# A new order for the opening of an attention and gated-unit kernel, with buffers named in the plan

## The chip, the cores and the metric

The kernel runs on one core of a Trainium2 chip. A core has five engines that run their own instruction queues side by side: TensorE (PE, matrix products, written to PSUM), VectorE (DVE), ScalarE (ACT), GpSimd (POOL) and SyncE (SP, which here only issues DMA transfers). PEld in a profile is TensorE's loading of weights. The metric is the device time of one execution in microseconds (us). Before the change, the median of 3 runs is 304.27 us (304.13 to 304.36).

## What is computed

Eight batches of attention without softmax, normalised per head, feed a causal gated unit:

```python
kv = np.einsum('bhsd,bhse->bhde', k, v)          # 8 batches, 8 heads, 576 tokens, 64 wide
out = np.einsum('bhsd,bhde->bhse', q, kv)
rms = np.sqrt(np.mean(out * out, axis=-1, keepdims=True) + 1e-06)
x = out / rms * g_norm                            # then (b, s, h*d): 576 tokens x 512
for k in range(5):
    gate_pre += conv_w[k] * xp[:, k:k + S, :]     # causal convolution, xp is x padded in front
gate = 1 / (1 + np.exp(-gate_pre))
return (gate * (x @ w_val)) @ w_out
```

q, k, v and g_norm are 32-bit floats as they arrive; w_val, conv_w and w_out arrive as 64-bit words, which the kernel stages as pairs of 32-bit words and narrows itself.

## The kernel before, in words

The program is a list of about 1,240 small steps, the string `PLAN`. The last loop of the kernel walks through it and calls one function per step; each function issues a few instructions to one engine, or DMAs to one queue. There is no scheduler behind it: each engine executes its instructions in the order in which the plan has them, and waits only for data it reads and for buffers that others still use. So the place of a step in the plan sets what it is queued behind on its own engine, and nothing else does.

The tokens of a batch are split into chunks 0 to 3 of 128 tokens and chunk 4 of 64. The steps that matter for the opening, with their lines in the kernel before:

- `load_q_rows`, `load_half`, `stage_weight` issue loads: q by rows (L331; qs), halves of k and v (L312), weights as they arrive (L346). Batch 0's v and half of its q go through ACT's queue, the convolution weights (`cw`) through POOL's, all else through SP's.
- `start_warm n 256` issues n products of the identity with itself (L433), which nothing reads.
- `turn_q_rows b j` transposes chunk j of q on PE (L485 for batch 0, L491 for batch 1); `sort_q b j` copies it from PSUM into `qT`: four copies for batch 0 (L504, on DVE for chunks 1 and 2, on ACT for the others), one ACT copy for batch 1 (L500).
- `kv_product b i` forms half i of k^T v on PE (L445); for batch 0 `kv_half` copies it with four ACT copies into the block-diagonal `kv_bd` (L455), for batch 1 `kv_copy` copies it whole (L459).
- `narrow_weight w j n` is part n of narrowing weight tile j. Parts 0 (L365), 5 (L382) and 6 (L387) run on DVE and need only the staged words; parts 1, 2, 3 (L370, L372, L374) are an ACT chain behind part 0; parts 4 (L377) and 7 (L391) run on DVE. Part 7 of `wval` multiplies by the column `gcol`.
- `turn_cw` transposes the narrowed convolution weights together with g_norm on PE (L416) and `keep_cw` takes `cwT` (the taps) and `gcol` out of that PSUM bank with three DVE instructions (L420 to L422).
- `raw_half 0 c i` multiplies chunk c of q by half i of `kv_bd` (L533). A chunk's raw product is whole when both halves are in its bank. `square` (ACT, L552), `sums` (DVE, L565), `powers` (POOL, L573) and `normalise` (DVE for batch 0, L582) make x; `turn_x` (PE, L604) and `keep_x` (ACT, L611) put it into `xT` with tokens along the row. Batch 1 and later use `raw_pair` and `raw_tail` (L521), squares of L556 and ACT's normalise (L592).
- `halo` (POOL, L632) copies the ends of the blocks of `xT` that the convolution needs; `gate_start` (ACT, L636), `gate_tap` (DVE, L642) and `gate_end` (ACT, L649) make the gate; `val_product` and `keep_val` (PE L654, ACT L663) the value product of batches 0 and 1, `gated` (DVE, L667) their product. From batch 2 on, `val_fast` and `val_keep` (L703 to L724) and `fast_product` and `fast_keep` (L795, L805 to L818) form products from seven block products each in place of eight.

The order around the change is this part of the plan before; a number after a name is a batch, a chunk, a half or a part:

```python
turn_q_rows 0 3; turn_q_rows 0 2; turn_q_rows 0 0; turn_q_rows 0 1; turn_q_rows 0 4; sort_q 0 3; ...
narrow_weight cw 0 2; narrow_weight cw 0 3; start_warm 3 256; kv_product 0 0; sort_q 0 1; kv_half 0 0;
sort_q 0 4; narrow_weight cw 0 4; narrow_weight cw 0 7; start_warm 1 256; raw_half 0 3 0; raw_half 0 2 0;
raw_half 0 0 0; kv_product 0 1; turn_cw; keep_cw; kv_half 0 1; raw_half 0 1 0; raw_half 0 4 0;
```

Buffers that are used again come from pools: `psum.tile(..., tag="bank", bufs=8)` hands out the eight PSUM banks in turn, and other tags do the same in SBUF (`ot` 3 buffers, `gate` 3, `x` 2, `wexp` 2, `w64` 3). A step that takes a buffer waits until the last reader of what was in it is done.

Of the kernel before, what the change touches and what calls it, by code (L numbers as in the profile page):

```python
# [15 lines left out]
P = 128  # L16
# [3 lines left out]
load_q_rows 0 1; stage_weight cw 0; load_q_rows 0 0; load_half v 0 0; load_half k 0 0; load_half v 0 1;  # L20
load_half k 0 1; warm_up; stage_weight wval 1; stage_weight wval 0; start_warm 5 256; turn_q_rows 0 3;
turn_q_rows 0 2; turn_q_rows 0 0; turn_q_rows 0 1; turn_q_rows 0 4; sort_q 0 3; sort_q 0 2;
narrow_weight cw 0 5; narrow_weight cw 0 6; narrow_weight cw 0 0; sort_q 0 0; narrow_weight cw 0 1;
narrow_weight cw 0 2; narrow_weight cw 0 3; start_warm 3 256; kv_product 0 0; sort_q 0 1; kv_half 0 0;
sort_q 0 4; narrow_weight cw 0 4; narrow_weight cw 0 7; start_warm 1 256; raw_half 0 3 0; raw_half 0 2 0;
raw_half 0 0 0; kv_product 0 1; turn_cw; keep_cw; kv_half 0 1; raw_half 0 1 0; raw_half 0 4 0;
narrow_weight wval 1 5; narrow_weight wval 1 0; raw_half 0 3 1;
load_q_rows 1 1; narrow_weight wval 1 1; narrow_weight wval 1 6; narrow_weight wval 1 2; raw_half 0 4 1;
raw_half 0 2 1; load_q_rows 1 0; narrow_weight wval 0 0; narrow_weight wval 0 5; square 0 3; stage_weight wval 3;
narrow_weight wval 0 6; narrow_weight wval 1 3; sums 0 3; load_half k 1 0; square 0 2; square 0 4;  # L30
narrow_weight wval 0 1; narrow_weight wval 1 4; sums 0 2; narrow_weight wval 0 2; raw_half 0 0 1; raw_half 0 1 1;
powers 0 3; sums 0 4; narrow_weight wval 1 7; normalise 0 3; square 0 1; square 0 0; sums 0 1; sums 0 0;
turn_q_rows 1 2; turn_q_rows 1 0; turn_q_rows 1 3; narrow_weight wval 0 3; sort_q 1 0; turn_x 0 3;
turn_q_rows 1 4; sort_q 1 2; turn_q_rows 1 1; keep_x 0 3; narrow_weight wval 3 0; load_half v 1 0;
stage_weight wval 2; load_half k 1 1; load_half v 1 1; powers 0 2; sort_q 1 3; normalise 0 2;
narrow_weight wval 3 1; narrow_weight wval 0 4; normalise 0 4; narrow_weight wval 0 7; narrow_weight wval 3 5;
stage_weight wout 1; load_q 2 0; stage_weight wout 0; powers 0 1; turn_x 0 4; narrow_weight wval 3 2;
turn_x 0 2; load_half k 2 0; kv_product 1 0; load_q 2 2; stage_weight wout 2; normalise 0 0; normalise 0 1;
narrow_weight wval 3 3; keep_x 0 2; keep_x 0 4; narrow_weight wval 3 4; narrow_weight wval 2 0; turn_x 0 0;
narrow_weight wval 3 6; turn_x 0 1; val_product 0 1 1; keep_x 0 0; kv_product 1 1; keep_x 0 1;  # L40
narrow_weight wval 3 7; narrow_weight wval 2 5; gate_start 0 0; val_product 0 3 1; gate_start 0 3;
narrow_weight wval 2 1; halo 0; sort_q 1 4; kv_copy 1 1; sort_q 1 1; kv_copy 1 0; gate_start 0 1;
narrow_weight wval 2 2; raw_pair 1 3; gate_tap 0 0 3; gate_tap 0 0 2; gate_tap 0 3 3; narrow_weight wval 2 3;
gate_tap 0 3 2; gate_tap 0 0 1; narrow_weight wout 1 0; narrow_weight wout 1 5; narrow_weight wval 2 6;
narrow_weight wval 2 4; load_half v 2 0; load_half k 2 1; load_q 2 1; square 1 3; narrow_weight wout 1 1;
narrow_weight wout 1 2; raw_tail 1; load_half v 2 1; keep_val 0 1 1; val_product 0 0 0; square 1 2;
narrow_weight wval 2 7; keep_val 0 3 1; gate_tap 0 3 1; sums 1 3; gate_tap 0 0 0; narrow_weight wout 0 0;
gate_tap 0 1 3; sums 1 2; turn_q 2 0; powers 1 3; keep_val 0 0 0; gate_end 0 0; val_product 0 2 1;
val_product 0 0 1; powers 1 2; load_q 2 3; narrow_weight wout 1 3; square 1 4; normalise 1 3; sums 1 4;
narrow_weight wout 1 6; narrow_weight wout 1 4; gate_tap 0 1 2; keep_val 0 0 1; val_product 0 1 0; raw_pair 1 1;  # L50
normalise 1 2; powers 1 4; turn_x 1 3; square 1 0; val_product 0 2 0; narrow_weight wout 1 7; gated 0 0;
gate_tap 0 1 1; keep_val 0 1 0; normalise 1 4; narrow_weight wout 0 1; sums 1 0; gate_start 0 2; turn_x 1 4;
turn_x 1 2; val_product 0 3 0; square 1 1; keep_x 1 4; keep_x 1 3; keep_x 1 2; narrow_weight wout 0 5;
gate_tap 0 3 0; val_sums 0; narrow_weight wout 2 5; narrow_weight wout 2 0; powers 1 0; gate_tap 0 2 3;
gate_tap 0 2 2; narrow_weight wout 0 2; gate_tap 0 2 1; sums 1 1; narrow_weight wout 0 3; keep_val 0 2 0;
keep_val 0 3 0; keep_val 0 2 1; stage_weight wout 3; narrow_weight wout 0 4; narrow_weight wout 0 6;
gate_tap 0 1 0; narrow_weight wout 2 6; gate_end 0 3; kv_product 2 0; normalise 1 0; powers 1 1;
val_product 1 0 1; halo 1; val_product 1 1 1; kv_product 2 1; turn_x 1 0; normalise 1 1; keep_val 1 0 1;
turn_q 2 2; narrow_weight wout 0 7; gate_tap 0 2 0; gate_end 0 1; gate_end 0 2; val_sums 1; turn_q 2 1;
gated 0 3; gated 0 2; turn_x 1 1; val_product 1 3 1; load_q 3 0; keep_x 1 0; turn_q 2 3; load_q 3 1;  # L60
load_half v 3 0; load_half v 3 1; narrow_weight wout 2 1; kv_copy 2 1; keep_x 1 1; weight_sums 0; val_sums 2;
gate_start 1 1; val_product 1 1 0; kv_copy 2 0; keep_val 1 1 1; narrow_weight wout 2 2; gate_tap 1 1 3;
keep_val 1 3 1; narrow_weight wout 2 3; narrow_weight wout 3 0; raw_pair 2 3; narrow_weight wout 3 5;
gate_tap 1 1 2; gated 0 1; square 2 2; square 2 3; keep_val 1 1 0; gate_start 1 0; narrow_weight wout 3 1;
raw_pair 2 1; val_product 1 0 0; narrow_weight wout 3 2; val_product 1 3 0; narrow_weight wout 3 3;
narrow_weight wout 3 6; token_sums 0 0 0; sums 2 3; val_product 1 2 1; val_product 1 2 0; powers 2 3; sums 2 2;
turn_q 3 0; token_sums 0 0 1; narrow_weight wout 3 4; square 2 1; keep_val 1 0 0; keep_val 1 3 0; load_q 3 3;
narrow_weight wout 3 7; narrow_weight wout 2 4; narrow_weight wout 2 7; load_half k 3 0; load_q 3 2;
load_half k 3 1; powers 2 2; fast_product 0 0 0; sums 2 1; normalise 2 3; token_sums 0 0 2; turn_blocks 2 3;
normalise 2 2; square 2 0; turn_q 3 1; powers 2 1; gate_start 1 3; fast_product 0 1 0; fast_product 0 0 1;  # L70
fast_keep 0 0 0; keep_val 1 2 0; normalise 2 1; weight_sums 1; raw_tail 2; sums 2 0; gate_tap 1 0 3;
fast_keep 0 0 1; fast_product 0 0 2; fast_keep 0 0 2; powers 2 0; square 2 4; keep_val 1 2 1; fast_keep 0 1 0;
weight_sums 2; token_sums 0 0 3; fast_product 0 0 3; fast_product 0 0 5; turn_blocks 2 2; turn_blocks 2 1;
sums 2 4; fast_keep 0 0 5; gate_tap 1 0 2; normalise 2 0; fast_product 0 0 4; fast_product 0 1 2; powers 2 4;
fast_keep 0 1 2; store 0 0; normalise 2 4; turn_blocks 2 0; move_blocks 2 0; move_blocks 2 2; move_blocks 2 1;
kv_product 3 0; fast_keep 0 0 4; turn_q 3 2; gate_tap 1 0 1; gate_tap 1 0 0; weight_sums 3; turn_q 3 3;
fast_product 0 1 4; turn_x 2 4; fast_product 0 1 1; kv_product 3 1; keep_x 2 4; kv_copy 3 0; kv_copy 3 1;
fast_product 0 0 6; move_blocks 2 3; raw_pair 3 3; raw_pair 3 1; gate_tap 1 3 3; load_half v 4 0; load_q 4 0;
gate_end 1 0; fast_keep 0 1 1; square 3 3; fast_keep 0 0 6; square 3 1; fast_product 0 1 3; fast_product 0 1 5;
gate_tap 1 3 2; gated 1 0; fast_keep 0 1 4; gate_tap 1 1 1; val_fast 2 0 0; sums 3 3; sums 3 1; gate_tap 1 1 0;  # L80
fast_keep 0 1 5; square 3 0; fast_product 0 1 6; square 3 2; sums 3 2; x_sums 2 0; gate_end 1 1; val_fast 2 1 0;
powers 3 3; x_sums 2 1; x_sums 2 3; gate_tap 1 3 1; gate_tap 1 3 0; val_fast 2 0 1; val_keep 2 0 0;
val_fast 2 0 2; x_sums 2 2; val_sums 3; sums 3 0; gated 1 1; fast_keep 0 1 6; val_keep 2 1 0; normalise 3 3;
val_keep 2 0 2; powers 3 2; powers 3 1; gate_end 1 3; val_fast 2 1 2; val_fast 2 1 1; load_half k 4 0;
val_keep 2 1 2; gate_start 1 2; val_keep 2 0 1; val_fast 2 0 4; gate_tap 1 2 3; val_keep 2 1 1; gate_tap 1 2 2;
val_fast 2 1 4; val_fast 2 0 5; val_fast 2 1 5; load_half v 4 1; normalise 3 2; load_half k 4 1; val_keep 2 0 4;
# [783 lines left out]
```

## Time and profile before

| what | value |
|---|---|
| median of 3 runs | 304.27 us |
| the profiled execution's own time | 305.54 us |
| its span, first to last instruction | 303.8 us |
| granted TensorE clock, mean | 0.995 |
| PE busy | 293.9 us (97% of the span) |
| DVE busy | 273.0 us (90%) |
| ACT busy | 194.4 us (64%) |
| POOL busy | 114.5 us (38%) |
| DMA | 55.51 MB, mean 183 GB/s |

The span is 1.7 us shorter than the profiled execution's own time; what lies around it is start and end of the program. The busy times are unions of instructions, so two that overlap count once. PE's busy time includes the products of `start_warm`, and a matmul that waits for its weights in mid-stream still counts as busy. In a timeline line stand the start, the time covered, the engine, the source line, the operation, what it writes and reads, and how many instructions are merged; a bracket gives the idle time before it and what ended that.

### The profile page before, as it was taken

What the parts mean: (1) busy time and instruction counts of PE and PEld (TensorE: products, weight loads), DVE (VectorE), ACT (ScalarE), POOL (GpSimd) and SP (SyncE); (2) the same over time, 40 slices, a digit from 0 to 9 for tenths busy, and PEclk for the clock granted to TensorE, in tenths of its full rate; (3) what the DMA queues carried; (4) which work ended last, traced back from release to release, by engine and by line L of the source; (5) the groups of instructions that cost most, each with busy time, mean ns of one, the idle gap of its engine ahead of it and who ended that gap; (6) DMA issues with size and microseconds to landing.
All of it is one profiled execution on the core that took longest, in us unless ns stands there. A gap on an engine that the chain in (4) does not pass through costs nothing.

```text
span 303.8 us, 8778 instructions
## 1 busy us (share of the span) xinstructions
PE 293.9 (97%) x3333; PEld 226.6 (75%) x3333; DVE 273.0 (90%) x482; ACT 194.4 (64%) x606; POOL 114.5 (38%) x127
## 2 busy tenths in 40 slices
PE   7998999999999999999999999999999999999993
PEld 4787777777887885777778757787877578888582
DVE  1699999999999999999999999999999999999612
ACT  2799989989568654983586537682888354534220
POOL 3047074326549036265328452245535613000000
PEclk9999999999999999999999999999999999999997
DMA  7999995277559776988589477937411621112423
GB/s 269 397 398 340 271 296 144 58 242 223 165 134 332 212 187 147 286 233 247 153 249 299 125 175 214 311 101 222 108 38 37 175 68 36 35 46 61 104 69 104
DMA packets 32073, 55.51 MB, mean 183 GB/s; under 512 B 6166, under 2 KB 14358, under 8 KB 32032
## 3 DMA queue, kind: packets, MB, share of 16 engines
q1 hardware_dynamic: 29520, 49.76, 56.6%
q0 software_dynamic: 1632, 3.17, 4.0%
q10 hardware_dynamic: 880, 2.03, 1.8%
q8 instruction: 26, 0.43, 0.6%
q14 instruction: 15, 0.12, 0.1%
HBM read 39.21 MB, written 9.44 MB: 160 GB/s over the span
## 4 chain that ended last, share of the span: by engine, by line
PE 76%; DMA 8%; SPq 5%; ACT 4%; DVE 3%; issue 2%; DVEq 0%
PE a L795 15%; PE va L703 13%; PE cb L795 12%; PE val L654 11%; PE vc L703 6%; PE kvps L445 4%; PE raw L521 4%; DMA out_dram<-ot 4%; PE out L741 4%; PE vb L703 3%; DMA qs<-in_q_dram 3%; SPq L625 2%; PE xTps L604 2%; DMA v<-in_v_dram 2%; SPq L322 1%
## 5 line engine op out<-in xcount | busy, mean ns | idle before, releaser
L573 POOL TENSOR_TENSOR rt<-ss,mhalf 128x8 f32<-128x8 f32 (+3 forms) x38 | 68.5, 1810 | 101.0 <-DVE ss L565 100.8
L642 DVE SCALAR_TENSOR_TENSOR gate<-xT,cwT,gate 128x576 f32<-128x576 f32 x128 | 101.8, 809 | 1.0
L592 ACT ACTIVATE x<-raw,rt 128x64 f32<-128x64 f32 x252 | 55.9, 353 | 6.9 <-POOL rt L573 4.1
L625 POOL DMA_DIRECT2D xT<-y x48 | 26.4, 557 | 25.9 <-DVE ot L805 14.4
L654 PE MATMUL val<-xT,wval 128*128 128x288 f32 x128 | 33.4, 412 | 0.0
L795 PE MATMUL a<-wsum,sums 128*128 128x256 f32 x128 | 32.5, 383 | 0.0
L649 ACT ACTIVATE gate<-gate 128x576 f32<-128x576 f32 x32 | 22.0, 692 | 12.1 <-DVE gate L642 11.9
L654 PEld LDWEIGHTS val<-xT,wval 128*128 128x128 f32 x128 | 23.5, 190 | 6.9 <-DVE wval L391 0.5
L795 PEld LDWEIGHTS a<-wsum,sums 128*128 128x128 f32 x128 | 23.9, 190 | 4.4 <-issue 0.6
L556 ACT ACTIVATE sq<-raw 128x256 f32<-128x256 f32 (+1 forms) x70 | 22.1, 402 | 7.8 <-PE raw L521 7.5
L703 PE MATMUL va<-xs,vsum 128*128 128x288 f32 x96 | 26.6, 409 | 0.0
L636 ACT ACTIVATE gate<-xT,cwT 128x576 f32<-128x576 f32 x32 | 25.2, 810 | 1.4 <-DVE gv L667 1.3
L565 DVE TENSOR_REDUCE ss<-sq 128x8 f32<-128x520 f32 (+1 forms) x40 | 24.7, 627 | 0.8 <-ACT sq L556 0.7
L667 DVE TENSOR_TENSOR gv<-gv,gate 128x576 f32<-128x576 f32 x32 | 23.6, 750 | 0.9 <-ACT gate L649 0.8
L703 PEld LDWEIGHTS va<-xs,vsum 128*128 128x128 f32 x96 | 18.0, 190 | 5.2 <-ACT x L592 0.4
L632 POOL COPY xT<-xT 128x124 f32<-128x124 f32 x32 | 17.5, 585 | 10.9 <-ACT xT L611 10.9
L521 PEld LDWEIGHTS raw<-kv,qT 64*64 64x64 f32 x1008 | 16.7, 134 | 6.4 <-issue 3.5
L521 PE MATMUL raw<-kv,qT 64*64 64x64 f32 x1008 | 19.0, 221 | 0.9 <-DVE gv L710 0.6
L445 PEld LDWEIGHTS kvps<-v,k 64*64 64x64 f32 x1008 | 15.8, 135 | 4.1 <-issue 2.9
L445 PE MATMUL kvps<-v,k 64*64 64x64 f32 x1008 | 17.4, 220 | 0.0
L470 DVE STREAM_TRANSPOSE qT<-qs 128x512 f32<-128x512 f32 x24 | 16.6, 693 | 0.5 <-DMA qs<-in_q_dram 0.5
L805 DVE TENSOR_TENSOR ot<-cb,ot 128x512 f32<-128x512 f32 x16 | 10.9, 681 | 6.8 <-DMA out_dram<-ot 4.1
(114 smaller groups left out, 545.5 us busy)
## 6 DMA issues: line engine op xcount, KB each, us to landing
qs<-in_q_dram SPq DMA_DIRECT2D x96, 140.0 KB, 4.6
out_dram<-ot SPq DMA_DIRECT2D x140, 64.0 KB, 1.7
k<-in_k_dram SPq DMA_DIRECT2D x14, 576.0 KB, 6.7
v<-in_v_dram SPq DMA_DIRECT2D x12, 576.0 KB, 7.0
xT<-y SPq DMA_DIRECT2D x48, 64.0 KB, 2.7
xT<-y POOLq DMA_DIRECT2D x48, 64.0 KB, 3.1
y<-in_moe_w_val_dram SPq DMA_DIRECT2D x4, 512.0 KB, 11.4
w_wout<-in_moe_w_out_dram SPq DMA_DIRECT2D x4, 512.0 KB, 7.1
```

Source lines behind the costliest of these rows:

```text
L445: nc.tensor.matmul(st["kvps", b][s][r * D:(r + 1) * D, i], st["k", b, i][rows, r, cols], st["v", b, i][rows, r, cols], start=(j == 0), sto ...
L521: nc.tensor.matmul(st["raw", b, c][r][cols, to * D:(to + 1) * D], st["qT", b][rows, hp, first:first + D], kvs[b % 2][rows, hp, :], start=T ...
L565: nc.vector.reduce_sum(out=st["ss", b][:, FIRST[c]:FIRST[c] + n], in_=st["sq", b, c][:, 0:n], axis=AX.X)
L573: nc.gpsimd.tensor_tensor(out=st["rt", b][:, which], in0=st["ss", b][:, which], in1=mhalf[:, which], op=ALU.pow)
L592: nc.scalar.activation(out=x[:, to * D:(to + 1) * D], in_=raw[:, h * D:(h + 1) * D], func=AF.Copy, scale=root[:, to:to + 1])
L625: (nc.sync if i % 2 else nc.gpsimd).dma_start(out=xTs[b % 2][i * TB:(i + 1) * TB, :, first:first + P], in_=y[a * TB:(a + 1) * TB, i])
L636: nc.scalar.activation(out=gate[:], in_=xTs[b % 2][:, jt, HALO:SX], func=AF.Copy, scale=cwT[:, K - 1, jt:jt + 1])
L642: nc.vector.scalar_tensor_tensor(out=gate[:], in0=xTs[b % 2][:, jt, tap * TB:tap * TB + S], scalar=cwT[:, tap, jt:jt + 1], in1=gate[:], op ...
L654: nc.tensor.matmul(val[:], wval[:, kc, jt * P:(jt + 1) * P], xTs[b % 2][:, kc, HALO + n * SV:HALO + (n + 1) * SV], start=(kc == 0), stop=( ...
L667: nc.vector.tensor_tensor(out=both, in0=both, in1=st["gate", b, jt][:], op=ALU.mult)
L703: nc.tensor.matmul(st[bank, "val", b, mj][:], weights_[:, k], tokens()[:, k], start=(n in (0, 1, 3) and k == 0), stop=(k == NK // 2 - 1), ...
L795: nc.tensor.matmul(st[bank, i, p], tokens()[:, k], weights_[:, k], start=(n < 2 and k == 0), stop=(k == NK // 2 - 1), skip_group_check=True)
```

## The change

Two things change. First, the plan: it has the same steps, each as often as before, in another order. In the opening, chunk 1 of q is turned first and chunks 3 and 2 last; `turn_cw` stands ahead of `kv_product 0 1` in place of behind it, and `keep_cw` right behind that product; the sort of chunk 3 stands behind the first `kv_half`; all raw halves stand behind `kv_product 0 1`, the two halves of chunk 4, of chunk 0 and of chunk 1 next to each other; the loads of batch 1 and of the weights change places on SP's queue, and `halo 0` stands ahead of three of the `keep_x 0` steps. Later parts of the plan are re-ordered as well, nearly everywhere by a few places; the last stores keep their queues.

Second, the buffers: the pools are replaced by tiles that are made once, and a step that takes a buffer names which one behind an `@`. The number of buffers of each kind stays. The warming products take a bank of their own each time, where they shared one before.

```diff
-turn_q_rows 0 2; turn_q_rows 0 0; turn_q_rows 0 1; turn_q_rows 0 4; sort_q 0 3; sort_q 0 2;
-narrow_weight cw 0 5; narrow_weight cw 0 6; narrow_weight cw 0 0; sort_q 0 0; narrow_weight cw 0 1;
-narrow_weight cw 0 2; narrow_weight cw 0 3; start_warm 3 256; kv_product 0 0; sort_q 0 1; kv_half 0 0;
-sort_q 0 4; narrow_weight cw 0 4; narrow_weight cw 0 7; start_warm 1 256; raw_half 0 3 0; raw_half 0 2 0;
-raw_half 0 0 0; kv_product 0 1; turn_cw; keep_cw; kv_half 0 1; raw_half 0 1 0; raw_half 0 4 0;
...
+stage_weight cw 0 @ 0; turn_q_rows 0 1 @ 1; turn_q_rows 0 4 @ 0; sort_q 0 1 @ 0; turn_q_rows 0 0 @ 2;
+sort_q 0 4; turn_q_rows 0 3 @ 3; turn_q_rows 0 2 @ 4; sort_q 0 0; start_warm 3 256 @ 0; load_q_rows 1 1;
+load_q_rows 1 0; narrow_weight cw 0 0 @ 0; narrow_weight cw 0 5 @ 0; narrow_weight cw 0 1; sort_q 0 2;
+stage_weight wval 3; kv_product 0 0 @ 1 2; narrow_weight cw 0 2; load_half k 1 0; narrow_weight cw 0 3;
+load_half v 1 0; start_warm 1 256 @ 0; narrow_weight cw 0 6 @ 1; narrow_weight cw 0 4; kv_half 0 0;
+narrow_weight cw 0 7; sort_q 0 3; turn_cw @ 4; kv_product 0 1; keep_cw; load_half k 1 1; stage_weight wval 2;
+raw_half 0 3 0 @ 3; narrow_weight wval 1 5 @ 1; kv_half 0 1; load_half v 1 1; narrow_weight wval 1 0 @ 0;
+raw_half 0 2 0 @ 4; narrow_weight wval 1 6 @ 0; narrow_weight wval 1 1; raw_half 0 3 1;
+narrow_weight wval 0 5 @ 2; raw_half 0 2 1; stage_weight wout 1 @ 0; square 0 3 @ 0;
+narrow_weight wval 0 6 @ 1; raw_half 0 4 0 @ 1; narrow_weight wval 1 2; sums 0 3 @ 0 0; raw_half 0 4 1;
+square 0 2 @ 1; raw_half 0 0 0 @ 2; narrow_weight wval 0 0 @ 1; stage_weight wout 0 @ 1; powers 0 3;
+square 0 4 @ 0; raw_half 0 0 1; sums 0 2; narrow_weight wval 1 3; raw_half 0 1 0 @ 0; sums 0 4; square 0 0 @ 1;
+raw_half 0 1 1; narrow_weight wval 1 4; turn_q_rows 1 2 @ 5; load_q 2 2; square 0 1 @ 0; sums 0 0; powers 0 2;
...
-    loads = ctx.enter_context(tc.tile_pool(name="loads", bufs=2))
-    work = ctx.enter_context(tc.tile_pool(name="work", bufs=2))
+    ROOMS = {"w64": (3, 1024), "ot": (3, 512), "wexp": (2, 512), "gate": (3, 576), "xs": (4, 576), "x": (2,
+             512), "qT": (2, 2304), "k0": (1, 1152), "k1": (1, 1152), "v0": (1, 1152), "v1": (1, 1152), "ss": (2,
+             36), "rt": (2, 36), "sq": (2, 520)}
+    rooms = {tag: [const.tile([P, size], FP32, name=f"{tag}_{n}") for n in range(count)]
+             for tag, (count, size) in ROOMS.items()}
+    rooms["bank"] = [psum.tile([P, 512], FP32, name=f"bank{n}") for n in range(8)]
+    picked = []
+    def new(tag, shape, dtype, name):
+        room = rooms[tag][picked.pop(0)]
...
     def ps(shape, name):
-        return psum.tile(shape, FP32, tag="bank", bufs=8, name=name)
+        return new("bank", shape, FP32, name)
...
         for step in PLAN.split(";"):
+            step, _, places = step.partition("@")
             name, *args = step.split()
+            picked[:] = [int(n) for n in places.split()]
             steps[name](*[int(a) if a.isdigit() else a for a in args])
```

Two switches that the diff adds change nothing here: `ACT_SUMS` is empty, and `PAIRED_Q` holds batch 0 as `WHOLE` did.

## The prediction, as it was put on record

> **What bounds the kernel now.** I read the page first, then the windows, the waits, and the timelines of the opening. The page's chain of waits is TensorE (PE) work for three quarters; the busy row beside it says the same, with VectorE (DVE) close behind:
>
> ```profile
> PE 293.9 (97%) x3333; PEld 226.6 (75%) x3333; DVE 273.0 (90%) x482; ACT 194.4 (64%) x606; POOL 114.5 (38%) x127
> ...
> PE 76%; DMA 8%; SPq 5%; ACT 4%; DVE 3%; issue 2%; DVEq 0%
> ```
>
> An average hides the stages, so I cut the span into windows (columns: length, then busy time and count of PE, PEld, DVE, ACT, POOL; granted clock; DMA share; GB/s):
>
> ```profile
> 8.00:16.00 8.00, 7.92 (x178) 5.87 (x177) 4.95 (x17) 6.04 (x21) 0.00 (x0) 1.00 1.06 398
> 16.00:24.00 8.00, 7.08 (x84) 5.97 (x83) 7.72 (x16) 7.34 (x14) 4.51 (x3) 1.00 1.05 398
> ...
> 28.60:64.00 35.40, 35.02 (x603) 27.05 (x601) 35.19 (x62) 32.98 (x96) 12.42 (x12) 1.00 0.74 198
> 64.00:176.00 112.00, 111.31 (x1422) 86.21 (x1423) 110.15 (x190) 78.11 (x272) 56.34 (x63) 1.00 0.76 215
> 176.00:284.00 108.00, 107.50 (x866) 83.79 (x864) 103.92 (x169) 60.62 (x187) 35.39 (x40) 1.00 0.42 114
> 284.00:298.70 14.70, 14.65 (x68) 10.60 (x64) 5.11 (x10) 3.00 (x8) 0.00 (x0) 1.00 0.33 85
> ```
>
> From 28.6 to 298.7 us PE is idle for 0.38+0.69+0.50+0.05 = 1.6 us in all: there the kernel is bound by PE, whose instructions the change keeps in number and shape. DVE is nearly as full there (idle 0.2 of 35.4 us, then 1.9 of 112). After 298.7 come 5.1 us of last copy and stores, which keep their engines and order. What can be moved is when the full stretch begins. PE before it:
>
> ```profile
> 12.01 1.83 PE L533 MATMUL raw<-kvbd,qT 128*128 128x128 f32 x12
> 13.77 1.28 PE L445 MATMUL kvps<-v,k 64*64 64x64 f32 x72
> 14.98 0.23 PE L416 MATMUL cwps<-ident,cw 21*128 21x21 f32 x1
> 15.14 4.05 PE L533 MATMUL raw<-kvbd,qT 128*128 128x128 f32 x28
> 19.12 2.84 PE L491 MATMUL qTps<-ident,qs 128*64 128x128 f32 x48
> 22.42 0.63 PE L604 MATMUL xTps<-ident,x 128*128 128x128 f32 x4 [0.46 <-ACT sq L552]
> 23.51 1.58 PE L491 MATMUL qTps<-ident,qs 128*64 128x128 f32 x24 [0.47 <-ACT qT L500]
> 25.65 0.85 PE L604 MATMUL xTps<-ident,x 128*128 128x128 f32 x6 [0.56 <-ACT wexp_wval L370]
> 26.43 1.28 PE L445 MATMUL kvps<-gv 64*64 64x64 f32 x72
> 27.64 1.11 PE L604 MATMUL xTps<-ident,x 128*128 128x128 f32 x8
> 28.58 2.11 PE L654 MATMUL val<-xT,wval 128*128 128x288 f32 x8
> ```
>
> The first value product starts at 28.58; before it PE waits three times (0.46+0.47+0.56) for the normalisation chain. That chain is late because DVE stood still: the convolution weights were ready at 12.51, but their turning sat on PE behind three raw halves and the second k^T v:
>
> ```profile
> 12.23 0.28 DVE L391 SCALAR_TENSOR_TENSOR cw<-ot_cw,wexp_cw 20x128 f32<-20x128 f32 x1
> 15.25 0.16 DVE L420 TENSOR_SCALAR gcol<-cwps 128x1 f32<-128x1 f32 x1 [2.73 <-PE cwps L416]
> ...
> 15.78 0.42 DVE L382 TENSOR_SCALAR ot_wval<-y 128x512 uint32<-128x512 uint32 x1
> ```
>
> **The change part by part**, times from the span's start; instructions of a kind are equal in number, so I walk the new order with the durations of these rows.
>
> *First loads and turned q.* The first eleven loads keep their queues and order; q lands at 6.0 to 6.2 and PE starts at 6.05. Chunk 1 is turned first and sorted by DVE from 7.2 (4 x 0.43) to 8.95. ACT sorts the small chunk 4 (4 x 0.27) and chunk 0 (4 x 0.375) from 7.5 to 10.1. The weight loads are in by then (issued 2.68, 5.8 us to landing). ACT's three weight steps (0.43 apart) end at 11.4; DVE does its first two, chunk 2 (1.73), then its last three, and ends at 12.06 against 12.51.
>
> *Turning the weights ahead of the second k^T v.* PE waits for them to 12.1. Behind that wait stands the second k^T v, whose k half lands at 12.09 (issued 1.68, 10.4 us); v's landing isn't told, but its other half took 0.2 us longer than k's (8.1 against 7.9), so I take 12.3. Bounds: nothing, or, if v lands only at 13.77, where the row above used it, some 1.5 us on this product and, less ACT's cover below, about 1 us on the end. I take nothing. keep_cw (three short rows, 0.62 from 15.25 to 15.87) runs 12.35 to 12.97, and DVE's next work waits for the value weights, landing at 2.19+11.2 = 13.4 and 2.98+11.7 = 14.7: a new wait of 0.4, in place of 2.7. DVE starts on them 2.4 us earlier (13.4 against 15.78).
>
> *Chunk 3's sort behind kv_half.* On ACT: kv_half 0 to 12.35 (4 x 0.22), chunk 3's sort to 13.88, kv_half 1 (0.87) to 14.77, against 15.97. The first raw half therefore waits to 13.95, against 12.01. This is the change's cost: PE idles 0.45 and has done no raw half before the second k^T v.
>
> *Raw halves in a row.* Ten halves at 0.57 (28 records in 3.98) are 5.7 us: 13.95 to 19.65, against an end of 19.12. PE is 0.5 later, yet chunk 3 is whole at 15.7 instead of about 16.8, and its square comes at 15.8 instead of 18.07, the last square ends at 20.2 instead of 22.3. POOL's three powers (2.07, 2.32, 2.89) end near 24.4 instead of 26.65; DVE's last normalise near 26.4 instead of 27.97.
>
> *PE to the value product.* From 19.65: 72 records of turned q at 0.059 (4.26), 18 of turned x at 0.117 (2.1, from 8 in 0.94) and one k^T v (1.21) are 7.57: 27.2. ACT has, from 20.2, three steps for weight 0 (0.75+0.65+0.63), three sorts (0.47 each), three steps of weight 3 (0.65+0.6+0.65) and three copies of turned x (0.5+0.35+0.5): 6.7, to 26.9. So PE, ACT and DVE meet within half a microsecond, and the three PE waits vanish because the chain is now 1.5 to 2.3 us earlier. The value product starts at 27.2: 28.58-27.2 = **1.4 us won**. What is late next is PE's own work.
>
> *Loads moved on SP's queue.* k and v of batch 1 and two value weights change places, the first two output weights go ahead of q of batch 2. DMA share is over 1.0 up to 48 us, so no load comes sooner by itself. The tightest: v's second half landed at 17.06+10.7 = 27.8, wanted at 29.2; the first output weight at 18.37+12.0 = 30.4, wanted by DVE near 31.6. I cost this at nothing; a slip past these margins costs its excess.
>
> *Halo 0 on POOL* moves ahead of three copies of x, to about 25.8, beside DVE's weight 3. In before it ran at 27.87, and the DVE row beside it took 0.81 where it takes 0.68: 0.13 each, three or four rows, 0.5 us of DVE, which is 1.5 us ahead.
> The Trainium skill, SBUF — State Buffer, section "SBUF: two separate sides", speaks against this: DVE work with two SBUF inputs and GpSimd work that reads SBUF share a port pair, and the loser "fully blocks". By it the four halo copies (2.1 us) would hold DVE outright; the 0.81 us row and the powers, beside which rows kept their 0.68, say they do not.
>
> *Everything after, and the places.* Both the rest of the order and the buffers are new: PSUM banks were taken in turn by a pool, now each has a number written out. Reading the list, a dozen banks are rewritten after only 0.86 to 1.2 us of PE work. An ACT copy takes 0.37 and the idle before it up to 0.22, so each fits with 0.3 to spare. The trace doesn't show these picks: at best all 1.6 us of PE idle go; at worst a dozen waits of 0.2 to 0.6 (PE's longest such wait is 0.6, a raw product waiting for DVE) cost 2.4 to 7 (the far end only if ACT is behind at all of them). I take zero, the row nearest: PE was stalled 1.6 us in 270.
>
> **Sum.** The profiled execution took 305.54 with a span of 303.8; the median of the runs is 304.27. Span 303.8-1.4 = 302.4; on the median 304.27-1.4 = **302.9 us**.
>
> **Rivals.**
> - *Middle gains too* (302.9-1.6 = 301.3): DVE gains 2.4 us of start against PE's 1.4, so the PE waits on DVE could go. For: the 0.6 wait is on DVE. Against: most of the rest is handover.
> - *The gain is given back* (304.3): DVE and ACT are 99% and 93% full up to 64 us; if a tight step there comes late, PE catches up with them. The halo as a full block belongs here: 2.1 us off DVE's 1.5 us lead leaves 304.3 or so. By that skill page this would be the outcome; the 0.13 says otherwise, so it has little weight.
> - *Slower: a hand-picked bank is still being read* (304.3-1.4+2.4 = 305.3 for twelve waits of 0.2). It decides once ACT's backlog passes 0.3 us at these places. For: the picks are tight. Against: ACT is only 56 to 70% busy after 64 us.
> - *It does not do what it says* (304.3): the weights are turned early, but DVE finds no value weights; against it stands their landing at 13.4.
>
> **Chances.** Forecast 0.42 (302.3 to 303.6), middle gains 0.23, given back 0.13, does nothing 0.04, slower 0.18. A measurement of this kernel tells about 0.2% (0.6 us) from no change. Faster 0.65, within 0.17, slower 0.18. The range reaches from 301.2 (all PE waits gone) to 305.3 (twelve bank waits); beyond it lie about 2 in 10.
>
> **What would show it.** In the changed profile: the weights' matmul near 12.1 and before the second k^T v; DVE's first value-weight row at 13.4; the last raw half at 19.6; no PE idle of 0.4 or more between 19.6 and 27; the value product at 27.2; PE idle from there to its end still near 1.6. A value product after 28 breaks the walk; PE waits on ACT copies after 64 us would be the slower rival.

## The result, and the profile after

| kernel | median | runs | ratio to before, 95% interval |
|---|---|---|---|
| before | 304.33 us | 303.71 to 304.63 (8) | |
| after | 305.53 us | 304.57 to 306.31 (8) | 1.0041, 1.0024 to 1.0058 |

The change makes the kernel 0.4% slower: 1.2 us lost where 1.4 were forecast as won, and just above the range. Two executions among the runs below, one of plan_pools (499.36 us, granted clock 0.56, the profiled one) and one of before (339.08 us, 0.853), are left out of the comparisons. The profiled execution of after took 305.46 us, with a span of 303.6. Its busy row and its chain of waits, from the page:

```profile
PE 292.6 (96%) x3333; PEld 226.0 (74%) x3333; DVE 273.0 (90%) x482; ACT 194.5 (64%) x606; POOL 112.5 (37%) x127
...
PE 70%; DMA 12%; DVE 9%; SPq 4%; issue 2%; ACT 1%; DVEq 0%; ACTq 0%
```

The sums hardly differ from before's; what moved is the chain, where DVE and DMA have more and PE less. PE's timeline of the opening answers to the one shown in the prediction:

```profile
12.05 0.23 PE L451 MATMUL bank<-ident,cw 21*128 21x21 f32 x1
12.48 1.28 PE L476 MATMUL bank<-v,k 64*64 64x64 f32 x72 [0.20 <-DMA v<-in_v_dram]
13.89 4.63 PE L563 MATMUL bank<-kvbd,qT 128*128 128x128 f32 x40
19.46 2.84 PE L521 MATMUL bank<-ident,qs 128*64 128x128 f32 x48 [0.94 <-DMA qs<-in_q_dram]
...
27.22 2.11 PE L698 MATMUL bank<-xT,wval 128*128 128x288 f32 x8
```

The weights are turned at 12.05 (forecast 12.1), the raw halves start at 13.89 (13.95), the value product at 27.22 (27.2). So at these three places the opening did what was forecast, and the loss is behind it. The windows, columns as in the prediction:

```profile
28.60:64.00 35.40, 34.84 (x604) 27.40 (x604) 35.33 (x62) 32.78 (x96) 11.12 (x10) 1.00 0.77 220
64.00:176.00 112.00, 110.25 (x1414) 85.00 (x1415) 108.56 (x186) 76.89 (x270) 56.52 (x64) 1.00 0.74 211
176.00:284.00 108.00, 107.41 (x866) 83.69 (x864) 103.70 (x169) 60.79 (x186) 34.54 (x39) 1.00 0.42 113
```

From 64 to 176 us PE idles 1.75 us (0.69 before) and DVE 3.4 (1.9 before); the later stretches hardly differ. From 28.6 to 298.7 us PE idles about 3 us in all; the prediction's last sign was that it would stay near 1.6. PE's own list of waits (us in all, times, longest) names, after 64 us, two of 0.6 that before did not have, both on an ACT copy:

```profile
PE bank L747 <- ACT gv L758: 0.6, 1, 0.6
PE bank L838 <- ACT ot L850: 0.6, 1, 0.6
```

They look like the slower rival, a PSUM bank that ACT has not yet emptied. The first of them, on the timeline of after (L711 is `gated`, L680 `gate_start`, L758 the copy that empties a bank of the value product, L747 `val_fast`):

```profile
94.75 0.74 DVE L711 TENSOR_TENSOR gv<-gv,gate 128x576 f32<-128x576 f32 x1
...
95.53 0.77 ACT L680 ACTIVATE gate<-xT,cwT 128x576 f32<-128x576 f32 x1 [1.78 <-DVE gv L711]
96.21 0.68 ACT L758 COPY gv<-bank 128x288 f32<-128x288 f32 x2
96.34 1.67 DVE L686 SCALAR_TENSOR_TENSOR gate<-xT,cwT,gate 128x576 f32<-128x576 f32 x2 [0.84 <-ACT gate L680]
96.64 0.54 PEld L747 LDWEIGHTS bank<-xT,vsum 128*128 128x128 f32 x3 [1.10 <-ACT gv L758]
96.64 0.75 PE L747 MATMUL bank<-xT,vsum 128*128 128x288 f32 x2 [0.65 <-ACT gv L758]
```

Read upwards: PE waits for ACT's copy, which is late only because it stands behind a `gate_start` that waited 1.78 us for DVE to finish `gated`. That is an SBUF tile: gate (1, 2) (batch, column tile) is written into the tile of gate (1, 1), and `gated 1 1` is the last to read it. The bank is where the wait is seen, not where it comes from.

### The profile page after: what moved, and what is told of

It reads as the page before. It is cut to its first block, busy times and chain, and to the rows that moved or that the text cites. A ratio compares the mean times of both kernels' runs of the same rounds, so it can differ in the third digit from the quotient of the medians.

```text
span 303.6 us, 8765 instructions
## 1 busy us (share of the span) xinstructions
PE 292.6 (96%) x3333; PEld 226.0 (74%) x3333; DVE 273.0 (90%) x482; ACT 194.5 (64%) x606; POOL 112.5 (37%) x127
## 4 chain that ended last, share of the span: by engine, by line
PE 70%; DMA 12%; DVE 9%; SPq 4%; issue 2%; ACT 1%; DVEq 0%; ACTq 0%
PE bank L838 29%; PE bank L747 23%; DMA qs<-in_q_dram 9%; PE bank L785 5%; PE bank L698 4%; PE bank L551 4%; DVE gate L686 3%; PE bank L476 3%; DMA k<-in_k_dram 2%; SPq L669 2%; DMA out_dram<-ot 2%; PE bank L648 1%; SPq L358 1%; PE bank L521 1%; PE bank L515 1%
## 5 line engine op out<-in xcount | busy, mean ns | idle before, releaser
L617 POOL TENSOR_TENSOR rt<-ss,mhalf 128x8 f32<-128x8 f32 (+3 forms) x38 | 68.0, 1794 | 100.3 <-DVE ss L607 100.3
L636 ACT ACTIVATE x<-bank,rt 128x64 f32<-128x64 f32 x252 | 55.8, 359 | 6.3 <-POOL rt L617 4.1
L838 PE MATMUL bank<-wsum,w 128*128 128x256 f32 x192 | 48.9, 385 | 0.9 <-ACT ot L850 0.6
L838 PEld LDWEIGHTS bank<-wsum,w 128*128 128x128 f32 x192 | 35.4, 190 | 8.8 <-DVE w L816 1.1
L747 PE MATMUL bank<-xs,vsum 128*128 128x288 f32 x144 | 38.1, 408 | 0.0
L669 POOL DMA_DIRECT2D xT<-y x48 | 26.4, 557 | 27.2 <-ACT ot L852 13.7
L838 PE MATMUL bank<-wout,gv 128*128 128x256 f32 x128 | 33.0, 384 | 0.3 <-ACT x L636 0.3
L698 PE MATMUL bank<-xT,wval 128*128 128x288 f32 x128 | 32.8, 409 | 0.0
L747 PEld LDWEIGHTS bank<-xs,vsum 128*128 128x128 f32 x144 | 27.1, 190 | 7.4 <-ACT x L636 0.4
L698 PEld LDWEIGHTS bank<-xT,wval 128*128 128x128 f32 x128 | 23.7, 190 | 6.1
L600 ACT ACTIVATE sq<-bank 128x256 f32<-128x256 f32 (+1 forms) x70 | 21.9, 390 | 9.0 <-PE bank L551 8.6
L747 PE MATMUL bank<-xT,wval 128*128 128x288 f32 x96 | 26.8, 411 | 0.5 <-DMA out_dram<-ot 0.2
L838 PEld LDWEIGHTS bank<-wout,gv 128*128 128x128 f32 x128 | 23.8, 190 | 4.4 <-ACT x L636 0.5
L680 ACT ACTIVATE gate<-xT,cwT 128x576 f32<-128x576 f32 x32 | 25.0, 807 | 3.1 <-DVE gv L711 3.1
L711 DVE TENSOR_TENSOR gv<-gv,gate 128x576 f32<-128x576 f32 x32 | 23.6, 751 | 1.0 <-ACT gate L693 0.8
L747 PEld LDWEIGHTS bank<-xT,wval 128*128 128x128 f32 x96 | 17.7, 190 | 5.0 <-issue 0.7
```

The costliest lines, as they stand in the source:

```text
L617: nc.gpsimd.tensor_tensor(out=st["rt", b][:, which], in0=st["ss", b][:, which], in1=mhalf[:, which], op=ALU.pow)
L636: nc.scalar.activation(out=x[:, to * D:(to + 1) * D], in_=raw[:, h * D:(h + 1) * D], func=AF.Copy, scale=root[:, to:to + 1])
L669: (nc.sync if i % 2 else nc.gpsimd).dma_start(out=xTs[b % 2][i * TB:(i + 1) * TB, :, first:first + P], in_=y[a * TB:(a + 1) * TB, i])
L680: nc.scalar.activation(out=gate[:], in_=xTs[b % 2][:, jt, HALO:SX], func=AF.Copy, scale=cwT[:, K - 1, jt:jt + 1])
L698: nc.tensor.matmul(val[:], wval[:, kc, jt * P:(jt + 1) * P], xTs[b % 2][:, kc, HALO + n * SV:HALO + (n + 1) * SV], start=(kc == 0), stop=( ...
L711: nc.vector.tensor_tensor(out=both, in0=both, in1=st["gate", b, jt][:], op=ALU.mult)
```

## The experiments

Each theory below was held before its runs. **Places:** the hand-picked PSUM banks lose the opening's gain and more (the rival of the prediction). **Rest:** the new order of the rest loses it. **Code:** tiles made once make waits that pool tiles don't. **SBUF:** the hand-picked SBUF tiles lose it. Two facts of the plans make clean cuts possible: the first 213 steps of both plans are the same set, so an opening of one can be joined to the rest of the other; and the places that the pools take can be read from the addresses in a built program and written behind the steps as `@` numbers. (They also correct a sentence above: the pools don't hand out in turn. Of the gates' tiles and of those of the tag `ot`, which outputs share with weight parts, they always gave the one whose last reader stands earliest in the plan: 29 and 51 picks.) The runs fall into four groups. Each group timed before anew (medians 304.05 to 304.27), and each ratio is to before in the same group; so differences of medians across groups are good to some tenths.

**before_again**, before unchanged.

> The kernel before, unchanged, to look at the base of the sum again: the profiled execution of before was 305.54 us (span 303.8), 1.2 us above the median of its own timed runs (304.3). If that execution was an untypical one (theory base), a second profile has a span near 302.5, the 1.2 us are found as waits of PE that the second profile does not have, and the loss of the changed kernel is to be looked for against the second profile. If profiling itself costs about 1.2 us here, the second profile is again 303.8 and the time 304.3. In both cases the ratio is 1.000.

304.27 us, ratio 1.0003 (0.9987 to 1.0019); its profiled execution took 306.40, with the first value product at 30.16 us, against 28.58 in the profile that the prediction used and 28.18 in a profile of the same opening that took 304.57 us (rest_pools, next). So profiling costs nothing by itself, but two of two profiles of before were executions 1.2 and 2.1 us above the median. By the one profile of this opening near the median, the base of the prediction's walk was some 0.4 us late at the value product.

**open_pools** and **rest_pools**, the two orders apart, all in pools.

```diff
 # open_pools
-PLAN of before, steps 1 to 213
+PLAN of after, steps 1 to 213, without places
 # rest_pools
-PLAN of before, steps 214 to the end
+PLAN of after, steps 214 to the end, without places
```

> Before with the changed kernel's order for its first 213 steps alone (the two orders have issued the same set of steps there), pools and the rest of the order as before. Theory places (the opening's 1.4 us are real, and the hand-picked PSUM banks lose them and more): 302.9 us, ratio 0.9955. Theory rest (the new order of the rest loses them, whatever the places): also 302.9. Theory given back (the early start is lost at the join, as DVE and the loads are not ahead): 304.3, ratio 1.000. If the opening itself costs: 305.5.

> Before with its own first 213 steps and then the changed kernel's order, in pools. Theory places: 304.3 us, ratio 1.000, since the order of the rest is innocent. Theory rest: 306.9 us (304.3 + 1.2 lost in all + 1.4 that the opening had won), ratio 1.009. Theory given back: 305.5, ratio 1.004.

open_pools 302.51 us, ratio 0.9943 (0.9927 to 0.9960); rest_pools 304.34, 1.0001 (0.9991 to 1.0011). The opening wins 1.8 us, the rest's order is worth nothing either way. Theory rest falls, for pools.

**banks_free**, the changed kernel with PSUM banks picked anew (125 steps differ), the bank that is longest free.

> The changed kernel with its order and its SBUF places, but with the PSUM bank of every step picked anew: the one whose last reader comes earliest in the order (125 steps get another bank). Theory places: PE's waits on banks between 64 and 176 us (1.75 us idle there, against 0.69 before) go, 303 to 304 us, ratio 0.996 to 0.999. Theory rest: 305.5 us, ratio 1.004, the same waits stay. A third outcome, slower than 305.5, would say that the hand-picked banks were better than a rule of longest free.

304.79 us, 1.0025 (1.0010 to 1.0040). The wait `PE bank L734 <- ACT gv L745: 0.6` is still there, under its new line numbers. These banks win 0.7 us, not the 3 that are missing between 302.5 and 305.5. (The new picks also bring a wait of 1.4 us of PE on DVE before the turned q of batch 1, in place of the 0.94 in after, so 0.7 is no upper bound.)

**plan_pools**, **pool_places**, **pool_banks**, **pool_sbuf**: the whole new order in pools; then the changed kernel's code with the pools' places for everything, for PSUM alone, for SBUF alone.

```diff
 # plan_pools: the code of before
+PLAN of after, without places
 # pool_places, pool_banks, pool_sbuf: the code and order of after, for instance
-val_product 0 1 1 @ 4; ... gate_start 1 2 @ 2; ... fast_keep 0 0 0 @ 0;
+val_product 0 1 1 @ 2; ... gate_start 1 2 @ 2; ... fast_keep 0 0 0 @ 1;
```

> Before's code with the changed kernel's whole order, every tile still from pools, no place picked by hand. Before with the new opening alone took 302.51 us and before with the new rest alone 304.34, so if both orders are innocent together: 302.5 us, ratio 0.994, and the whole loss of the changed kernel (3.0 us) is the fixed tiles and their places. If the two orders hurt each other: 304 to 305.5.

> The changed kernel's code (one fixed tile per place) and its whole order, but at every step the place that the pools of the previous kernel take, in PSUM and in SBUF. Theory places: as with pools, 302.5 us, ratio 0.994. Theory code (fixed tiles make waits that pool tiles do not make, wherever they lie): 305.5 us, ratio 1.004, although every tile lies where the pools put it.

> The changed kernel with the pools' PSUM banks and its own hand-picked SBUF places. Theory banks (my rival of the prediction): 302.5 to 303 us, ratio 0.995. Theory SBUF (the hand-picked tiles for outputs, gates, squares and normalised chunks are still being read or stored): 304.8 to 305.5, since picking the banks anew by the longest-free rule gave only 304.79. Theory code: 305.5.

> The changed kernel with its own hand-picked PSUM banks and the pools' SBUF places. Theory banks: 305.5 us, ratio 1.004. Theory SBUF: 302.5 to 303.5, ratio 0.995 to 0.998 (the bank picks may keep up to 0.7 us, the difference that picking them anew made). Theory code: 305.5.

| PSUM banks | SBUF tiles | median | ratio, 95% |
|---|---|---|---|
| pools (plan_pools) | pools | 302.73 | 0.9948, 0.9930 to 0.9966 |
| as the pools (pool_places) | as the pools | 303.10 | 0.9968, 0.9947 to 0.9990 |
| by hand (pool_sbuf) | as the pools | 303.52 | 0.9971, 0.9951 to 0.9991 |
| as the pools (pool_banks) | by hand | 305.27 | 1.0032, 1.0016 to 1.0048 |
| by hand (after) | by hand | 305.53 | 1.0041, 1.0024 to 1.0058 |

The time follows the SBUF column. Banks make 0.3 to 0.4 us, the fixed tiles as such 0.4, both within their intervals. Theories places (for PSUM) and code fall as main causes; SBUF stands.

**gates_free**, **outs_free**, **gates_outs_free**: which SBUF tiles. The pools' places for the tag `gate`, for the tag `ot`, for both; all else by hand.

```diff
 # gates_free
-gate_start 1 0 @ 0; ... gate_start 1 3 @ 1; ... gate_start 1 2 @ 2; ... gate_start 2 0 @ 0;
+gate_start 1 0 @ 2; ... gate_start 1 3 @ 0; ... gate_start 1 2 @ 2; ... gate_start 2 0 @ 1;
 # outs_free
-fast_keep 0 0 0 @ 0; ... fast_keep 0 1 0 @ 1; ... fast_keep 0 2 0 @ 1; ... fast_keep 0 2 1 @ 2;
+fast_keep 0 0 0 @ 1; ... fast_keep 0 1 0 @ 0; ... fast_keep 0 2 0 @ 2; ... fast_keep 0 2 1 @ 0;
```

> The changed kernel with one thing undone: the tile of each gate (28 of 32 picks differ) is the one that the pools take. In the changed kernel gate (1, 2) goes, at 95 us, into the tile of gate (1, 1), whose last reader stands only 7 steps earlier in the order; the pools take the tile of gate (1, 0), read 50 steps earlier. Theory gates (that one wait is passed on from ACT to DVE to ACT to PE): the stall of PE at 96 us goes and the time falls by 1 to 2 us, to 303.5 to 304.5, ratio near 0.999. Theory outputs: 305.5, ratio 1.004. Theory spread (many tags each a little): 305.0 to 305.3.

> The changed kernel with the pools' tiles for outputs and weight parts alone (the tag that 42 of 54 picks change). At 106 us output (0, 2) goes into the tile of output (0, 1), whose store is 27 steps earlier in the order; the pools take one 67 steps earlier. Theory outputs: the stall of PE at 107 us (0.98) goes, 304.5, ratio 1.001, and more if it carries on. Theory gates: 305.5, ratio 1.004. Theory spread: 305.0 to 305.3.

> Both of the two edits: gates and outputs where the pools put them, all else by hand. All of the pools' SBUF places took 303.52 us, all by hand 305.53. Theory gates and outputs together: 303.5 or below (the hand-picked tiles for normalised chunks let the value product start at 27.2 rather than at 28.2, so up to 1.0 below: 302.5), ratio 0.994 to 0.998. If the squares or the normalised chunks hold the loss: 305.

(The second expectation numbers outputs by pairs of token chunks; by single chunks, output 4 goes into the tile of output 2.) gates_free 305.40 us, 1.0036 (1.0011 to 1.0061); outs_free 305.16, 1.0025 (1.0007 to 1.0043); both together 303.79, 0.9992 (0.9972 to 1.0012). Either alone wins next to nothing (0.1 and 0.4 us, inside the intervals), both win 1.7 (1.5 by the ratios): the two waits stand one behind the other. In outs_free the stall at 107 us is gone and the one of 0.64 at 97 us stays. In gates_free the stall at 96 us is gone, and the one at 107 has grown (L837 writes the output tile, L803 is `token_sums`, L825 `fast_product`):

```profile
106.69 0.65 DVE L803 TENSOR_TENSOR w<-gv,w 128x512 f32<-128x512 f32 x1
...
106.93 0.37 ACT L837 COPY ot<-bank 128x256 f32<-128x256 f32 x1 [2.46 <-DMA out_dram<-ot]
...
107.35 0.73 PEld L825 LDWEIGHTS bank<-wsum,w 128*128 128x128 f32 x4 [2.10 <-ACT ot L837]
107.35 1.13 PE L825 MATMUL bank<-wsum,w 128*128 128x256 f32 x4 [1.70 <-DVE w L803]
```

ACT waits 2.46 us for a store to leave the output tile, and PE stands 1.70; in after it stood 0.65 at 96 us and 0.60 here, and ACT's wait between 86 and 118 us was shorter:

```profile
ACT ot L850 <- DMA out_dram<-ot: 1.4, 1, 1.4
```

(The bracket of PE's row names L803, which ended last, at 107.34. It can't be what PE waited for: in gates_outs_free the same product starts at 104.81, and that L803 row only at 105.93. The weight load's bracket names the copy.) ACT's copy comes at 106.93 in gates_free and at 107.13 in after, though PE reached this place 1.3 us sooner (its product before starts at 104.52 and 105.83). So the first stall had only given the store time. With both undone the gate starts without a wait and PE runs through (gates_outs_free, same steps as in the fence above):

```profile
92.79 0.78 ACT L667 ACTIVATE gate<-xT,cwT 128x576 f32<-128x576 f32 x1
...
93.46 0.69 ACT L745 COPY gv<-bank 128x288 f32<-128x288 f32 x2
93.88 0.74 DVE L698 TENSOR_TENSOR gv<-gv,gate 128x576 f32<-128x576 f32 x1
...
95.19 1.62 PE L734 MATMUL bank<-xT,vsum 128*128 128x288 f32 x6
```

Here the gate (L667) is begun before `gated` (L698), since it lies in a tile that was read long before. PE's start times tell the same (first record of each product, us):

| kernel | value product | first `val_fast` | first `out_product` | between the last two |
|---|---|---|---|---|
| rest_pools | 28.2 | 89.0 | 116.3 | 27.3 |
| open_pools | 27.8 | 87.4 | 114.9 | 27.5 |
| after | 27.2 | 87.2 | 117.2 | 30.0 |
| gates_free | 27.2 | 87.1 | 117.0 | 29.9 |
| outs_free | 27.3 | 87.6 | 116.5 | 28.9 |
| gates_outs_free | 27.1 | 86.5 | 113.9 | 27.4 |
| two_swaps (next) | 28.0 | 87.7 | 115.3 | 27.6 |

Nearly the whole loss against open_pools lies in these 30 us.

**two_swaps** and **hand_gates_outs**: are two picks enough, and does the loss come back?

```diff
 # two_swaps: after, with tiles 0 and 2 of gate exchanged from here on, and 1 and 2 of ot
-gate_start 1 2 @ 2; ... gate_start 2 0 @ 0; ... fast_keep 0 2 0 @ 1; ... fast_keep 0 2 1 @ 2;
+gate_start 1 2 @ 0; ... gate_start 2 0 @ 2; ... fast_keep 0 2 0 @ 2; ... fast_keep 0 2 1 @ 1;
 # hand_gates_outs: pool_places, with the tags gate and ot as in after
```

> The changed kernel with two picks undone and every later one kept as it was: from gate (1, 2) on, gate tiles 0 and 2 change names, and from output 4 of the first block on, output tiles 1 and 2. So only the two tight pairs are taken apart; all other relations of who follows whom on a tile stay by hand. Theory two picks: as with all gates and outputs from the pools, 303.8 us, ratio 0.999. Theory many picks: 305.2 to 305.5, ratio 1.004, with the stalls of PE at 96 and 107 us gone and new ones elsewhere.

> The reverse: everything where the pools put it (303.10 us so) but gates and outputs by hand. Theory gates and outputs: the stalls at 96 and 107 us come back, 305 to 305.9 us, ratio 1.003 to 1.005. If they hurt only beside the other hand-picked tiles: 303.1.

two_swaps 303.78 us, 0.9991 (0.9978 to 1.0004), the same as with all gates and outputs undone: the two picks are the cause of these 1.75 us (1.5 by the ratios). hand_gates_outs 305.05, 1.0036 (1.0021 to 1.0052), 1.95 above pool_places: the loss comes back. Its trace has the gate's stall again (`ACT gate L667 <- DVE gv L698: 1.8`, PE 0.6 at 97 us), but no wait for a store at 107: with the pools' banks this one didn't show, against my expectation. pool_banks and outs_free have the gate's stall alone too (0.65 and 0.64), and banks_free as well. So one of the two stalls is enough: every kernel of the new order whose trace shows either took 304.8 to 305.5 us, every one whose trace shows neither 303.1 to 303.8. How a stall of 0.6 us of PE goes with 1.4 to 2 us of time (305.16 against 303.79, 305.05 against 303.10) is not shown.

**mix**, gates, outputs and banks from the pools.

> The changed kernel with gates, outputs and PSUM banks from the pools, and the rest (normalised chunks, squares, value sums, weight parts' expansions) by hand: the version that should beat both kernels if each group counts by itself, as the hand-picked tiles let the value product start at 27.1 us (28.2 with the pools'). Theory additive: 302 to 302.8 us, ratio 0.993 to 0.996. If the bank picks make no difference: 303.8, ratio 0.999.

303.60 us, 0.9978 (0.9963 to 0.9993), not 302 to 302.8. That the groups add up is not borne out. The time is not told apart from two_swaps, pool_sbuf or pool_places, which lie from 303.1 to 303.8.

**turn_first** and **chunks_first**, the opening's own parts, in pools.

```diff
 # turn_first: before
-raw_half 0 3 0; raw_half 0 2 0; raw_half 0 0 0; kv_product 0 1; turn_cw; keep_cw;
+turn_cw; keep_cw; raw_half 0 3 0; raw_half 0 2 0; raw_half 0 0 0; kv_product 0 1;
 # chunks_first: open_pools
-turn_cw; kv_product 0 1; keep_cw; ... raw_half 0 0 0;
+kv_product 0 1; ... raw_half 0 0 0; turn_cw; keep_cw;
```

> Before with one part of the opening alone: the turn of the convolution weights and its keep stand ahead of the first raw halves and so ahead of the second k^T v; everything else as before. The whole new opening takes 302.51 us against 304.3. By the prediction the weights' conversion on VectorE starts 2.4 us earlier with the turn, and the join with the raw halves then limits: theory turn: 303 us, ratio 0.996, most of the gain. Theory chunk order (the halves in a row and the sort of chunk 3 make the gain): 304.3 or later, since the first raw halves now stand behind a turn that waits for the weights at 12.5 us: ratio 1.000 to 1.003.

> Before with the whole new opening (302.51 us) but the turn of the convolution weights and its keep back behind the first raw halves of three chunks, about where before has them. With the turn alone moved the time was 303.96 against 304.10, no gain. Theory both needed (the value product waits for the later of the weights and the raw products): 304 us, ratio 1.000. Theory chunk order alone: 302.5 to 303, ratio 0.995.

turn_first 303.96 us, 1.0002 (0.9982 to 1.0022): the turn alone wins nothing. chunks_first 303.39, 0.9984 (0.9969 to 0.9998): with the turn late, part of the gain of open_pools (302.51) remains. In turn_first PE waits 0.97 us before the turn (the first row below), its raw halves end 0.4 us later than in before, and the wait of 0.46 for a square is gone; from 22.41 us on its rows start as in before. The other two waits, and their sizes, are those of before:

```profile
12.67 0.21 PE L409 MATMUL cwps<-ident,cw 21*128 21x21 f32 x1 [0.97 <-ACT kvbd L448]
...
23.51 1.58 PE L484 MATMUL qTps<-ident,qs 128*64 128x128 f32 x24 [0.47 <-ACT qT L493]
25.65 0.85 PE L597 MATMUL xTps<-ident,x 128*128 128x128 f32 x6 [0.56 <-ACT wexp_wval L363]
```

In chunks_first the weights are turned at 17.13, yet neither of these two waits is there and the value product starts at 28.03. A wait on DVE's normalise stands in their place:

```profile
17.13 0.23 PE L409 MATMUL cwps<-ident,cw 21*128 21x21 f32 x1
...
22.72 0.63 PE L597 MATMUL xTps<-ident,x 128*128 128x128 f32 x4 [1.05 <-DVE x L575]
23.27 1.53 PE L484 MATMUL qTps<-ident,qs 128*64 128x128 f32 x24
24.73 0.87 PE L597 MATMUL xTps<-ident,x 128*128 128x128 f32 x6
```

Both waits of turn_first end on ACT, and it is the new order of chunks, sorts and narrowing steps that clears them. The early turn is worth something beside that order: open_pools lies 0.9 us below chunks_first by the medians and 1.2 by the ratios, whose intervals don't overlap. So neither of the two theories holds as it stands. No wait of 0.9 us in the traces accounts for it: open_pools waits 0.85 at the place of the 1.05.

## Why the prediction was wrong, point by point

- **The failing step: "Everything after, and the places … I take zero."** The nearest row was the wrong one. I looked through the PSUM banks, priced them, and put the slower rival there. The SBUF tiles were named in the same plan, and I left them out: they went into the sum at nothing without a reason. Two of them cost 1.75 us: a gate into a tile read seven steps before, an output into a tile whose store was still under way. They took back more than the forecast's 1.4. What is left between two_swaps (303.78) and plan_pools (302.73) is 1.05 us, made up of banks, other tiles and fixed tiles; no run tells them apart.
- **The slower rival** had the sign and almost the size (305.3), but not the mechanism. PE does wait on ACT copies after 64 us, as its sign said, yet changing the banks won 0.7 (banks_free) or 0.3 (pool_banks), and SBUF tiles alone 2.0 (pool_sbuf). ACT was no busier than I thought; it stood in its queue behind a step that waited.
- **Opening order, 1.4 us:** near in size. open_pools wins 1.8 (interval 1.2 to 2.2), and in after the walk held within 0.1 us at the weights, the raw halves and the value product. The last of these is in part luck, as two terms were off and cancelled: ten raw halves took 4.6 us, not 5.7, and PE then waited 0.94 for q of batch 1, a load that I had not followed.
- **Its cause was only a part.** "That chain is late because DVE stood still" is not enough: with the turn alone moved (turn_first) DVE is served early, at 13.51, and two of the three waits stay. Their brackets name a sort of q and a narrowing step on ACT, which I had read as the normalisation chain. The early turn wins nothing alone and 0.9 to 1.2 us beside the rest (302.51 against 303.39).
- **"Only the start moves":** half right. Against rest_pools the value product of open_pools is only 0.4 earlier, while the first `fast_product` is 1.4 earlier (70.3 against 71.7). The other 1.0 is won between 28 and 71 us: 0.4 is one wait that is gone (at 63.57 us), in the rest PE's records keep a closer pitch (32 records of `val_product` from 34.5 us take 8.03 us, 8.31 in rest_pools). That is the place of the rival "middle gains too", but not its mechanism, since no wait on DVE went; and it did not add to the sum. These are single profiles, whose times differ by some tenths.
- **The base:** the walk started from an execution that was 1.2 us slower than the median, and took its value product (28.58) for typical. By rest_pools it was nearer 28.2, so the move at this place was 1.0, not 1.4; that rests on one profile.
- **Loads moved, at nothing:** no wait for them but the 0.94 above and k of batch 2 (0.4 at 54 us), whose load stands later in the plan. PE's idle time there rose by 0.2 in 35 us.
- **Halo 0 earlier:** the DVE row behind it took its plain 0.68 us, not 0.81. By the Trainium skill, SBUF — State Buffer, section "SBUF: two separate sides", a DVE instruction with two SBUF inputs and a GpSimd instruction that reads SBUF contend for a port pair: whichever starts first holds it for the whole instruction, and the other "fully blocks". The rows agree: four halo copies took 0.98 us here beside DVE rows that read PSUM, and 1.97 at 92.6 us in after, beside a DVE row with two SBUF inputs that took 0.86 (mean 0.78). So most of the wait is POOL's, and DVE pays about 0.1 a row; that DVE would be held for all four was my reading of the rule, not what the rows show.

## What to carry to other kernels

When buffers are picked by hand, list for every pick how many steps lie between the last reader of the old content and the new writer, SBUF tiles and stores included: of two tight picks each looked harmless when undone alone (0.1 and 0.4 us), and both together cost 1.75. The count says where to look and no more: seven gate picks in pool_places (303.10 us) stand 3 to 7 steps behind the last reader, and from 28.6 us to the last product no single wait of PE there is above 0.33 us. A PE wait on a PSUM copy says who was late, not why; follow the engine that was late one step further back in its own queue. And change order and places in separate kernels: the order alone was worth 1.8 us won, and it was kept where pools gave out the buffers (302.51 and 302.73, the fastest here).

## What the runs showed of the hardware

- The raw halves ran closer in the new order: 40 records in 4.63 us (0.116 each), where 28 records in the order of before took 4.05 (0.145). The order of the halves is not all of it, since the first three halves of before, 12 records in 1.83 us, took 1.60 in the same order in turn_first. Why was not tried.
- In gates_free a store of an output held its tile until ACT had waited 2.46 us, to 106.93, though the transfers of this kind land 1.7 us (median in after) after issue: they were the last four of eight that SP issued from 100.3 to 105.5, about one in 0.66 us. ACT stood from 104.47 on, so 1.1 us of its wait passed before the last of them was issued, and 1.4 after.
